# A planned kernel of retention and two mixing layers: waits between GpSimd and VectorE, another load order, another ReLU path, a new plan

## The chip, the cores and the metric

The program runs on one core of one Trainium2 chip. The metric is device time in microseconds of one execution. The profiled execution is one of the same program; its trace gives start and end of every instruction on TensorE (PE, and PEld for its weight loads), VectorE (DVE), ScalarE (ACT), GpSimd (POOL) and the DMA queue that SyncE (SP) issues.

## What is computed

Retention over 768 positions (2 batches, 8 heads of 64), then a layer that mixes positions at low rank and channels with a ReLU between, then a layer with a gate whose other half is normalised and mixed over positions. Shortened:

```python
state = gamma * state + k_t v_t^T            # for t in 768 positions
y_t   = scale * q_t state
x = y as (batch, 768, 512)
u = x + (x^T @ U @ V)^T
x = u + relu(u @ w_ch1) @ w_ch2              # 512 -> 2048 -> 512
h = relu(x @ w_in); a, v = halves of h       # 512 -> 1024
v = (v - mean) / sqrt(var + 1e-6)
out = (a * (w_spatial @ v + b)) @ w_out
```

## The kernel before

The recurrence is done in six chunks of 128 positions. A *pair* is two heads of one batch, eight pairs in all, 0 to 3 of the first batch. For each pair TensorE makes scores (banks `sc`, from keys `k` and queries `q`, both feature-major), which are scaled and masked into `pt`, the chunk sums (`ds`, from token-major keys `kk` and values `v`), and VectorE scans these into states `s`. A masked tile is made in one of two ways: VectorE does it in one operation (line 451), or ScalarE scales (line 448) and GpSimd masks (line 449); the table `VIA` says which of a pair's four tiles (number 2h+e, half h of the positions, head e) go the second way. `x` then adds the products of `pt` and `v`, and of `s` and `q`. The tokens are turned (`t`, copied into `xtok`) for the low-rank product `g`, which is copied to `gt` and multiplied up again (`hu`), and the result is added to `x`.

All the later products are exact to about float32 by splitting: every operand is a high part (rounded by ScalarE) and a low part (a subtraction on VectorE or GpSimd), and each product is three matmuls (`triple`, line 348 for all matmuls). Weights arrive as 64-bit words and are converted in five operations: two on ScalarE (595, 596), two on VectorE (597, 598), one addition on GpSimd (600); then come the high part `hw` (608) and the low part `lw` (609). Activations are `f` (high and low in one tile), `a` in the channel layer. The first products of the channel layer (all but the first of eight blocks of 256 hidden channels), the gate's and the last ones go through a product of 2 by 2 blocks in seven multiplications (`quad`, banks `qa` to `qd`), with sums of weights and of activations; the second products of the channel layer (`acc`) are plain. `pz` are the products over positions, `qv` those of the normalised half, `qo` the last ones.

Nothing is ordered by hand. Every operation is recorded with the engines that may do it, their costs in ns, and a key (its due time in us); `Plan.arrange` goes through time, gives each engine the earliest operation that can start, and chooses between VectorE, GpSimd and ScalarE; `settle` repeats this 14 times with keys moved towards the latest possible times. `give_out` then writes the instructions in the order of planned start. Constants (`AT0`, `LEAD`, `SUM0` and the like) are due times. Each engine runs its list in that order, so an operation that waits holds all behind it on its engine. The planner assumes that VectorE and GpSimd operations marked True, those that read two inputs of SBUF, don't overlap; before, nothing in the program enforced which of the two goes first. Where the plan leaves TensorE idle for over 500 ns, `give_out` writes filler matmuls on a constant; `WARM` fillers start the program. The loads go out on SyncE's queue in the order of `LOADS`: `q`, `h` (the feature-major keys), `k` (the token-major keys), `v`, then `gs`, `U`, `V` and weights; up to eight are in flight. A pair in `TURNED` has no token-major load: TensorE transposes its keys (line 414) and VectorE and ScalarE scale them into `kk` (419).

Of the kernel before, what the change touches and what calls it, by code (L numbers as in the profile page):

```python
# [39 lines left out]
class Op:  # L40
    __slots__ = ("key", "eng", "fn", "bufs", "deps", "outs", "need", "start", "end", "seq", "size", "cost")


class Plan:
# [16 lines left out]
    def op(self, eng, fn, r=(), w=(), key=None, size=0):  # L61

        o = Op()
        o.key, o.eng, o.fn, o.size = (self.key if key is None else key), dict(eng), fn, size
# [28 lines left out]
    def arrange(self, sizes):  # L93
# [15 lines left out]
        dma, sent = 0.0, 0  # L109
        free["D"] = FIRST  # L110
# [17 lines left out]
        def span(o, e, t0):  # L128
# [20 lines left out]
        while given < len(order):  # L149
# [107 lines left out]
    def give_out(self, engines, pools, idle):  # L257

        free = 0.0
        for o in sorted(self.ops, key=lambda o: (o.start, o.seq)):  # L260
# [15 lines left out]
def vss(n):  # L276
    return 152 + 1.03 * n, True
# [22 lines left out]
def pe(n, passes=1):  # L300
    return passes * (10.8 + 0.4219 * n), False
# [3 lines left out]
POOLS = {"a": 36, "w": 24, "raw": 2, "y": 2, "t": 2, "r": 6, "st": 6, "s": 2, "g": 2, "sm": 2, "ps": 8}  # L305
# [5 lines left out]
WARM = 11  # L311
# [3 lines left out]
AT0, AT1, CH0, CH1 = 1.0, 20.7, 43.5, 22.3  # L315
STEP0, STEP1, UV = 4.9, 5.3, 21.6
LOADS = 'q0 h0 v0 k1 gs h1 v1 q1 q2 h2 k2 v2 q3 h3 k3 v3 U V0 V1 w10 w11 q4 h4 k4 v4 w20 w21 q5 h5 v5 k5 q6 k6 v6 q7 h6 v7 h7 k7'.split()
LEAD = 11.1
# [3 lines left out]
SUM0, SUM1 = 80.8, 106.2  # L322
VIA = {0: (2,), 1: (), 2: (), 3: (0, 1, 2, 3), 4: (2, 3), 5: (1, 2, 3), 6: (1, 2), 7: (1, 3)}
# [3 lines left out]
TURNED = (0,)  # L327
# [8 lines left out]
def tile_kernel(ctx: ExitStack, tc: tile.TileContext, a, out: bass.AP):  # L336
    nc = tc.nc
    const = ctx.enter_context(tc.tile_pool(name="const", bufs=1))
    psm = ctx.enter_context(tc.tile_pool(name="psm", bufs=1))
# [16 lines left out]
    sc_t = const.tile([P, 2 * H + NP * (NCH - 1)], F32, name="scales")  # L356
# [71 lines left out]
    def scores(i):  # L428
# [3 lines left out]
        for h in range(2):  # L432
# [8 lines left out]
            op({"P": (690, "keys")}, run, r=[(k_t[i], h), (q_t[i], h)], w=sc)  # L441
# [17 lines left out]
        op({"P": (600, "tokens")}, run, r=[(kk_t[i], 0), (kk_t[i], 1), v_t[i]], w=[ds])  # L459
# [3 lines left out]
    def mix(i):  # L463

        for h in range(2):
# [3 lines left out]
            for z, x in enumerate(xp):  # L469
# [5 lines left out]
                op({"P": (656, "tokens")}, intra, r=[v_t[i + z], (pt_t[i + z, 0], h), (pt_t[i + z, 1], h)], w=[x])  # L475
# [45 lines left out]
    def up(b):  # L521
        for h in range(2):
            for j in range(NP // 2):
# [6 lines left out]
                op({"P": (660, "up")}, run, r=[g_t[b], (vst, h)], w=u)  # L530
# [216 lines left out]
    def ch1(m, b):  # L747
        def store(i, h, src, add=None, y=None):
# [52 lines left out]
    def gate_v(b, c0):  # L801

        sm = Buf("sm", [P, 2, 16], F32, f"sm{b}{c0}")
# [78 lines left out]
    with tc.manual_schedule():  # L882
# [6 lines left out]

        def busy(n):  # L890
# [3 lines left out]
        dma(lambda: sc_t[:], lambda: a["sc"], P * 36 * 4, w=["sc"], eng="E")  # L894
# [7 lines left out]
        op({"A": (1500.0, False)}, lambda e: e.activation(psm.tile([P, 1], F32, name="table"), warm[:, 0:1], AF.Copy))  # L902
# [90 lines left out]
        plan.give_out({"P": None, "V": nc.vector, "A": nc.scalar, "G": nc.gpsimd, "D": nc.sync, "E": nc.scalar}, pools, spend)  # L993
# [70 lines left out]
```

## Time and profile before

| | us |
|---|---|
| three timed runs: lowest, median, highest | 455.47, 455.50, 456.25 |
| the profiled execution | 454.77 |
| its span in the trace | 453.1 |
| TensorE busy (share of the span) | 447.2 (99%) |
| VectorE busy | 396.3 (87%) |
| ScalarE busy | 257.0 (57%) |
| GpSimd busy | 126.7 (28%) |
| data read and written | 39.27 MB, 3.15 MB |

The span is about 1.7 us shorter than the execution it belongs to; the rest lies outside the traced instructions. The ends of matmuls are modelled and each overlaps the next, so a group's duration is a little more than the distance to the next group's start; starts are exact. An engine's idle time counts only where TensorE waits for what the engine makes.

### The profile page before, as it was taken

The numbers are of one execution on the slowest core, as the hardware profiler recorded it, in microseconds if no ns is written. First come the engines' busy times: TensorE is split into PE (matmuls) and PEld (weight loads), VectorE is DVE, ScalarE is ACT, GpSimd is POOL, SyncE is SP. The second block draws the span as 40 slices with busy tenths as digits, with TensorE's granted clock in tenths as the row PEclk, the third lists the DMA queues.
The fourth block names the chain that finished last, engine by engine and source line by source line (L and its number), as shares of the span: only waits on it lengthen the run. The fifth ranks groups of instructions, "written<-read, shape, count | busy, mean of one in ns | idle before, by whom it ended". The sixth has DMA issues, their size and how long they took to land.

```text
span 453.1 us, 8442 instructions
## 1 busy us (share of the span) xinstructions
PE 447.2 (99%) x3235; PEld 434.8 (96%) x3235; DVE 396.3 (87%) x847; ACT 257.0 (57%) x526; POOL 126.7 (28%) x112
## 2 busy tenths in 40 slices
PE   9999999999999999999999999999999999999996
PEld 6888799999999999999999999999999999999996
DVE  2767899999999999989888797899997999999843
ACT  3376775673766675754563554566566778353410
POOL 3076763463834242322131012101410001150000
PEclk9999999999999999999999999999999999999999
DMA  8995412320353341433122012000112022000033
GB/s 299 399 399 192 139 50 93 93 94 10 90 179 95 94 138 50 150 110 107 54 93 81 13 48 87 19 1 1 35 36 72 0 94 93 2 1 1 1 139 139
DMA packets 14151, 42.95 MB, mean 95 GB/s; under 512 B 1696, under 2 KB 2592, under 8 KB 14112
## 3 DMA queue, kind: packets, MB, share of 16 engines
q1 hardware_dynamic: 13968, 42.41, 27.3%
q8 instruction: 25, 0.41, 0.4%
q14 instruction: 14, 0.11, 0.1%
q10 hardware_dynamic: 144, 0.02, 0.0%
HBM read 39.27 MB, written 3.15 MB: 94 GB/s over the span
## 4 chain that ended last, share of the span: by engine, by line
PE 92%; DVE 5%; ACT 1%; POOL 0%; issue 0%; DVEq 0%; ACTq 0%
PE acc L348 29%; PE pz L348 8%; PE x L348 4%; PE c L348 4%; PE sc L348 3%; PE t L502 1%; PE ds L348 1%; DVE s21t L556 1%; DVE f21t L562 1%; PE idle L348 1%; DVE f21b L562 1%; DVE pz L862 1%; DVE x L863 1%; PE q10a L348 1%; PE q50a L348 0%; PE qo11d L348 0%
## 5 line engine op out<-in xcount | busy, mean ns | idle before, releaser
L348 PE MATMUL acc<-a,hw 128*128 128x384 f32 x512 | 130.1, 334 | 0.0
L348 PEld LDWEIGHTS acc<-a,hw 128*128 128x128 f32 x512 | 92.5, 188 | 0.3 <-DVE a L759 0.3
L348 PE MATMUL acc<-a,lw 128*128 128x384 f32 x256 | 85.5, 334 | 0.0
L784 DVE TENSOR_TENSOR x<-acc,x 128x384 f32<-128x384 f32 x128 | 69.3, 550 | 7.5 <-PE acc L348 6.9
L600 POOL TENSOR_TENSOR rw<-rw,tw 128x512 int32<-128x512 int32 x32 | 50.7, 1586 | 82.8 <-DVE rw L598 69.8
L348 PEld LDWEIGHTS acc<-a,lw 128*128 128x128 f32 x256 | 48.1, 188 | 0.0
L757 ACT ACTIVATE y<-y 128x384 f32<-128x384 f32 x42 | 22.0, 523 | 36.9 <-DVE y L756 36.7
L595 ACT ACTIVATE yw<-raww 128x512 f32<-128x512 f32 x32 | 21.6, 676 | 19.7 <-DVE rw L598 15.0
L759 DVE TENSOR_TENSOR a<-y,a 128x384 fp32r<-128x384 f32 x39 | 23.7, 608 | 2.9 <-ACT a L758 2.5
L598 DVE SCALAR_TENSOR_TENSOR rw<-yw,rw 128x512 uint32<-128x512 uint32 x32 | 23.1, 723 | 0.0
L596 ACT ACTIVATE tw<-raww 128x512 int32<-128x512 uint32 x32 | 21.6, 674 | 1.1 <-POOL rw L600 1.0
L600 POOL TENSOR_TENSOR rwo<-rwo,two 128x512 int32<-128x512 int32 x4 | 5.4, 1341 | 60.0 <-DVE rwo L598 60.0
L758 ACT CAST a<-y 128x384 fp32r<-128x384 f32 x42 | 21.5, 513 | 1.0
L449 POOL TENSOR_TENSOR pt<-pt,shared 128x384 f32<-128x384 f32 x14 | 14.2, 1036 | 18.7 <-ACT pt L448 18.6
L348 PE MATMUL pz<-ws,vn 128*128 128x384 f32 x108 | 19.0, 334 | 0.0
L348 PE MATMUL pz<-hws,vn 128*128 128x384 f32 x72 | 18.9, 334 | 0.0
L348 PEld LDWEIGHTS pz<-ws,vn 128*128 128x128 f32 x108 | 18.8, 188 | 0.0
L600 POOL TENSOR_TENSOR rwv<-rwv,twv 128x512 int32<-128x512 int32 x4 | 5.3, 1333 | 30.9 <-DVE rwv L598 12.6
L608 ACT CAST hw<-rw 128x512 fp32r<-128x512 f32 x18 | 11.1, 618 | 4.5 <-POOL rw L600 4.2
L348 PE MATMUL sc<-q,k 64*128 64x128 f32 x192 | 13.4, 281 | 0.0
L597 DVE TENSOR_SCALAR rw<-yw 128x512 uint32<-128x512 uint32 x32 | 13.4, 423 | 0.0
L348 PEld LDWEIGHTS sc<-q,k 64*128 64x128 f32 x192 | 11.7, 187 | 1.6 <-issue 0.7
(1080 smaller groups left out, 1260.6 us busy)
## 6 DMA issues: line engine op xcount, KB each, us to landing
raww<-in_w SPq DMA_DIRECT2D x32, 512.0 KB, 3.6
q<-in_qT SPq DMA_DIRECT2D x8, 384.0 KB, 7.8
k<-in_kT SPq DMA_DIRECT2D x8, 384.0 KB, 7.9
v<-in_v SPq DMA_DIRECT2D x8, 384.0 KB, 7.7
kk<-in_k SPq DMA_DIRECT2D x7, 384.0 KB, 7.8
raws<-in_ws SPq DMA_DIRECT2D x6, 384.0 KB, 3.0
out_y<-out SPq DMA_DIRECT2D x6, 384.0 KB, 2.4
rawwu<-in_wu SPq DMA_DIRECT2D x4, 512.0 KB, 3.5
```

Source lines behind the costliest of these rows:

```text
L348: nc.tensor.matmul(o, l, r, start=start, stop=stop, skip_group_check=True)
L449: op({"G": gss(T)}, lambda E, pt=pt: E.tensor_mul(pt(), pt(), tri()), r=[(pt_t[i, e], h), TRI], w=[(pt_t[i, e], h)])
L595: op({"A": c}, lambda E: E.activation(y.t, words(1).bitcast(F32), AF.Copy, scale=2.0 ** -112), r=whole, w=[y])
L596: op({"A": c}, lambda E: E.activation(t.t, words(0), AF.Copy, scale=2.0 ** -29), r=whole, w=[t])
L597: op({"V": vone(n)}, lambda E: E.tensor_single_scalar(r.t, y.t.bitcast(U32), 3, ALU.logical_shift_left), r=[y], w=[r])
L598: op({"V": vss(n)}, lambda E: E.scalar_tensor_tensor(r.t, y.t.bitcast(U32), 0x80000000, r.t, ALU.bitwise_and, ALU.bitwise_or), r=[y, r], w ...
L600: op({"G": gss(n)}, lambda E: E.tensor_tensor(o().bitcast(I32), r.t.bitcast(I32), t.t, ALU.add), r=[r, t], w=[tok])
L608: op({"A": acp(DM)}, lambda E: E.copy(h.t, f(r.t)), r=[r], w=[h])
L757: op({"A": (525, False)}, lambda E: E.activation(y[0](), y[0](), AF.Relu), r=[y[1]], w=[y[1]])
L758: op({"A": acp(T)}, lambda E: E.copy(t.t[:, 0, :], y[0]()), r=[y[1]], w=[(t, 0)])
L759: op({"V": vss(T), "G": gss(T)}, lambda E: E.tensor_sub(t.t[:, 1, :], y[0](), f(t.t[:, 0, :])), r=[y[1], (t, 0)], w=[(t, 1)])
L784: op({"V": vps(T)}, lambda E, o=o, v=xs(b, d, h): E.tensor_add(v, o.t, v), r=[o, ("X", b, d, h)], w=[("X", b, d, h)])
```

## The change

- A GpSimd operation marked as sharing with VectorE is made to wait for the last such VectorE operation that was planned in front of it, if that one was planned to end less than 3,000 ns ahead (`tie`). The planner also keeps 100 ns (`TIE`) between them, and all costs on VectorE, ScalarE and GpSimd are raised by 1% (`PAD`); some costs on TensorE are set anew.
- Pair 0's keys are the first load, its queries the second; pair 1 joins `TURNED`. The order of the other loads changes. Nine fillers start the program instead of eleven, and the count of later ones is rounded down.
- ReLU in the channel layer: before, ScalarE took the ReLU in place and then rounded the result into the high part, and the low part was a subtraction. Now ScalarE writes the ReLU straight into the high part, and VectorE makes the low part from the unclipped sum, with the ReLU in the same operation.
- The last block is added and stored in two halves, by the queues of ScalarE and SyncE.
- `w` has 23 buffers for 24 and `raw` 3 for 2; due times, `VIA` and so the whole order are new.

```diff
-                st = max(st, port[0])
+                st = max(st, port[0] + (TIE if e == "G" else 0.0))
...
+                    o.tie = sole if e == "G" and sole is not None and sole.end > st - NEARBY else None
+                    sole = o if e == "V" else sole
...
-                    idle(int((o.start - free - 200.0) / 320.0) + 1, target[-1])
+                    idle(int((o.start - free - 100.0) / 320.0), target[-1])
...
-            o.fn(engines[o.eng])
+            o.ins = o.fn(engines[o.eng])
+            if o.eng == "G" and o.cost[1] and o.tie is not None:
+                tie(o.ins, o.tie.ins)
...
-WARM = 11
+WARM = 9
-LOADS = 'q0 h0 v0 k1 gs h1 v1 q1 q2 h2 k2 v2 q3 h3 k3 v3 U V0 V1 w10 w11 ...
+LOADS = "h0 q0 v0 h1 gs q1 v1 q2 h2 v2 k2 h3 k3 q3 v3 U V0 V1 w10 w11 ...
-LEAD = 11.1
+LEAD = 13.9
-VIA = {0: (2,), 1: (), 2: (), ...
+VIA = {0: (2, 3), 1: (1,), 2: (0,), ...
-TURNED = (0,)
+TURNED = (0, 1)
...
-            op({"A": (525, False)}, lambda E: E.activation(y[0](), y[0](), AF.Relu), r=[y[1]], w=[y[1]])
-            op({"A": acp(T)}, lambda E: E.copy(t.t[:, 0, :], y[0]()), r=[y[1]], w=[(t, 0)])
-            op({"V": vss(T), "G": gss(T)}, lambda E: E.tensor_sub(t.t[:, 1, :], y[0](), f(t.t[:, 0, :])), r=[y[1], (t, 0)], w=[(t, 1)])
+            op({"A": (525, False)}, lambda E: E.activation(t.t[:, 0, :], y[0](), AF.Relu), r=[y[1]], w=[(t, 0)])
+            op({"V": vss(T)}, lambda E: E.scalar_tensor_tensor(t.t[:, 1, :], y[0](), 0.0, f(t.t[:, 0, :]), ALU.max, ALU.subtract), r=[y[1], (t, 0)], w=[(t, 1)])
...
+            if (b, m, i, h) == (B - 1, 1, 0, 1):
+                for z, q in enumerate("ED"):
+                    sl, to = slice(z * T // 2, (z + 1) * T // 2), slice(h * T + z * T // 2, h * T + (z + 1) * T // 2)
+                    op({"V": vps(T // 2)}, lambda E, sl=sl, to=to: E.tensor_add(t.t[:, to], src.t[:, sl], add[0]()[:, sl]), r=[src, add[1]], w=[(t, h, z)])
+                    dma(lambda to=to: out[b, d * P:(d + 1) * P, to], lambda to=to: t.t[:, to], P * T * 2, r=[(t, h, z)], eng=q)
...
+        def tie(late, early):
+            tc.add_manual_dep(late.ins, early.ins.name, mybir.DependencyInfo(mybir.DependencyClass.Sync, mybir.DependencyReason.DATA), reason="port")
```

How the order moves is shown at three places. First GpSimd's list at the start, from the copies of the decay factors to pair 3's masks (`pt` with pair and head; before first, then after):

```order
L385 COPY decay1_130<-scales_94 128x320 x2
L449 TENSOR_TENSOR pt00_187<-pt00_187,shared_111 128x384
L449 TENSOR_TENSOR pt30_415<-pt30_415,shared_111 128x384
L449 TENSOR_TENSOR pt31_428<-pt31_428,shared_111 128x384
L449 TENSOR_TENSOR pt30_415<-pt30_415,shared_111 128x384
```

```order
L392 COPY decay1_124<-scales_91 128x320 x2
L456 TENSOR_TENSOR pt00_173<-pt00_173,shared_96 128x384
L456 TENSOR_TENSOR pt01_177<-pt01_177,shared_96 128x384
L456 TENSOR_TENSOR pt11_262<-pt11_262,shared_96 128x384
L456 TENSOR_TENSOR pt20_308<-pt20_308,shared_96 128x384
L456 TENSOR_TENSOR pt30_409<-pt30_409,shared_96 128x384
```

Pair 0 now has two masks on GpSimd, and pairs 1 and 2 one each.

Second, VectorE's list where the second batch's additions of `hu1` meet the first weight tiles of the channel layer (`rw`, `lw10`, `lw11`; `s` and `f` are sums and splits of the first batch's activations):

```order
L533 TENSOR_TENSOR x1_96<-hu112_1008,x1_96 128x384
L533 TENSOR_TENSOR x1_96<-hu113_1009,x1_96 128x384
L609 TENSOR_TENSOR lw10_1059<-rw10_851,hw10_927 128x512
L562 TENSOR_TENSOR f00b121_968<-x0_95,f00b121_968 128x384
L556 TENSOR_TENSOR s00t3_1069<-x0_95 128x384
L562 TENSOR_TENSOR f00b221_974<-x0_95,f00b221_974 128x384
```

```order
L496 COPY xtok30_936<-t70_932 128x3x128
L616 TENSOR_TENSOR lw10_954<-rw10_887,hw10_944 128x512
L604 TENSOR_SCALAR rw20_983<-yw20_908 128x512
L604 TENSOR_SCALAR rw21_987<-yw21_923 128x512
L563 TENSOR_TENSOR s00t1_815<-x0_92 128x384
L605 SCALAR_TENSOR_TENSOR rw20_983<-yw20_908,rw20_983 128x512
L616 TENSOR_TENSOR lw11_1006<-rw11_889,hw11_985 128x512
L540 TENSOR_TENSOR x1_93<-hu100_1001,x1_93 128x384
```

The low part `lw10` stood behind the eight additions and now stands in front of them, as does `lw11`, which was GpSimd's before.

Third, VectorE's list in the last stretch, where the splits of the second batch's sums (`f21t`) end and the first sums of the output blocks (`yo`, from banks `qo`) begin:

```order
L562 TENSOR_TENSOR f21t20_5323<-s21t2_5313,f21t20_5323 128x384
L562 TENSOR_TENSOR f21t21_5362<-s21t2_5313,f21t21_5362 128x384
L562 TENSOR_TENSOR f21t40_5345<-s21t4_5336,f21t40_5345 128x384
L562 TENSOR_TENSOR f21t41_5372<-s21t4_5336,f21t41_5372 128x384
L694 TENSOR_TENSOR yo000_5330<-qo00b_5340,yo000_5330 128x384
L696 TENSOR_TENSOR yo001_5396<-qo00c_5353,yo000_5330 128x384
L873 TENSOR_TENSOR out001_5402<-qo00d_5326,yo001_5396 128x384
```

```order
L569 TENSOR_TENSOR f21t20_5278<-s21t2_5268,f21t20_5278 128x384
L569 TENSOR_TENSOR f21t21_5317<-s21t2_5268,f21t21_5317 128x384
L569 TENSOR_TENSOR f21t41_5327<-s21t4_5291,f21t41_5327 128x384
L701 TENSOR_TENSOR yo000_5285<-qo00b_5295,yo000_5285 128x384
L569 TENSOR_TENSOR f21t40_5300<-s21t4_5291,f21t40_5300 128x384
L703 TENSOR_TENSOR yo001_5351<-qo00c_5308,yo000_5285 128x384
L569 TENSOR_TENSOR f21b210_5170<-x1_93,f21b210_5170 128x384
L890 TENSOR_TENSOR out001_5361<-qo00d_5281,yo001_5351 128x384
```

The sum `yo001` now has one split behind it that stood in front, and one split stands between it and `yo000`.

## Rows read from the trace of the kernel before

**Rows 1.** The page, part 1: busy us (share of the span) xinstructions, by engine
```profile
PE 447.2 (99%) x3235; PEld 434.8 (96%) x3235; DVE 396.3 (87%) x847; ACT 257.0 (57%) x526; POOL 126.7 (28%) x112
```

**Rows 2.** Waits of TensorE's weight loads (PEld): us in total, times, longest
```profile
PEld c L348 <- POOL lw L609: 0.9, 1, 0.9
PEld hu L348 <- DVE gt L489: 0.7, 1, 0.7
...
PEld c L348 <- ACT hw L608: 0.7, 1, 0.7
...
PEld qo00c L348 <- DVE yo L696: 0.5, 1, 0.5
...
PEld qv02c L348 <- DVE yv L696: 0.4, 1, 0.4
...
PEld acc L348 <- DVE a L759: 0.3, 1, 0.3
PEld q10a L348 <- DVE lw11a L609: 0.2, 1, 0.2
```

**Rows 3.** Timeline of TensorE, 0 to 16 us: start, us, engine, line, operation, count
```profile
0.84 3.68 PE L348 MATMUL idle<-const-bfloat16-1.0 128*128 128x384 bf16 x11 [0.84 <-PEq L1053]
...
5.92 1.08 PE L414 MATMUL k<-shared,k 128*128 128x128 f32 x6
6.92 1.61 PE L348 MATMUL sc<-q,k 64*128 64x128 f32 x24
...
10.40 0.88 PE L348 MATMUL x<-pt,v 128*64 128x128 f32 x12
...
13.33 0.50 PE L348 MATMUL sc<-const-bfloat16-1.0 128*128 128x384 bf16 x2
13.77 1.61 PE L348 MATMUL sc<-q,k 64*128 64x128 f32 x24
```

**Rows 4.** DMA issues up to 1.3 us: KB each, median us to landing
```profile
q<-in_qT SPq DMA_DIRECT2D x1, 384.0 KB, 3.1
k<-in_kT SPq DMA_DIRECT2D x1, 384.0 KB, 3.6
```

**Rows 5.** Timeline of ScalarE and GpSimd, 8 to 10.5 us
```profile
8.56 0.58 ACT L448 ACTIVATE pt<-sc,scales 128x384 f32<-128x384 f32 x1 [1.11 <-PE sc L348]
...
9.30 1.00 POOL L449 TENSOR_TENSOR pt<-pt,shared 128x384 f32<-128x384 f32 x1 [3.52 <-ACT pt L448]
```

**Rows 6.** Timeline of TensorE, 56 to 59 us
```profile
56.81 0.59 PE L348 MATMUL c<-f00b,hw 128*128 128x384 f32 x2
57.96 0.44 PE L348 MATMUL c<-f00b,lw 128*128 128x384 f32 x1 [0.56 <-POOL lw L609]
```

**Rows 7.** Chain that ended last, 330 us to the end: start, us, what
```profile
371.04 36.42 PE pz L348 x210
...
407.48 0.57 DVE pz L862
...
424.88 1.88 DVE f21t L562 x4
```

**Rows 8.** Groups by line: names, shapes, count | busy us, mean ns | idle before
```profile
L489 ACT COPY xtok<-t 128x384 f32<-128x384 f32 x11 | 5.0, 481 | 6.6 <-PE t L502 6.5
...
L639 DVE TENSOR_TENSOR lsbw<-sbw,hsbw 128x512 fp32r<-128x512 f32 x7 | 4.8, 681 | 0.0
```

**Rows 9.** Timeline of GpSimd and VectorE, 83.7 to 86 us
```profile
83.73 1.55 POOL L600 TENSOR_TENSOR rw<-rw,tw 128x512 int32<-128x512 int32 x1 [0.63 <-DVE rw L598]
...
84.10 1.74 DVE L609 TENSOR_TENSOR lw11a<-rw,hw11a 128x512 fp32r<-128x512 f32 x1
```

**Rows 10.** The page, part 6: stores, KB each, median us to landing
```profile
out_y<-out SPq DMA_DIRECT2D x6, 384.0 KB, 2.4
out_y<-out SPq DMA_DIRECT2D x4, 192.0 KB, 1.9
```

**Rows 11.** Line 600, GpSimd's addition of 512: count, ns min/median/max
```profile
L600 POOL TENSOR_TENSOR rw<-rw,tw x32: 1284/1348/4427, 49.9 to 228.6; 128x512 int32<-128x512 int32 x32
```

More of the change, by code (lines that the diff above doesn't have):

```diff
@@ L40 @@
 class Op:
-    __slots__ = ("key", "eng", "fn", "bufs", "deps", "outs", "need", "start", "end", "seq", "size", "cost")
+    __slots__ = ("key", "eng", "fn", "bufs", "deps", "outs", "need", "start", "end", "seq", "size", "cost", "tie", "ins")
 class Plan:
@@ L63, in op @@
         o = Op()
-        o.key, o.eng, o.fn, o.size = (self.key if key is None else key), dict(eng), fn, size
+        o.key, o.eng, o.fn, o.size = (self.key if key is None else key), {e: (c * PAD if e in "VAG" else c, x) for e, (c, x) in eng.items()}, fn, size
         deps, bufs = {}, []
@@ L108, in arrange @@
         port, tiles = [0.0, None], False
-        dma, sent = 0.0, 0
-        free["D"] = FIRST
+        dma, sent, sole = 0.0, 0, None
+        free["D"], free["P"] = FIRST, FIRST
         def add(o):
@@ L255, in settle, with give_out @@
             go(best[1])
-    def give_out(self, engines, pools, idle):
+    def give_out(self, engines, pools, idle, tie):
         free = 0.0
@@ L300, in pe @@
 def pe(n, passes=1):
-    return passes * (10.8 + 0.4219 * n), False
+    return passes * (11.3 + 0.4219 * n), False
 NM = NF // 2
-POOLS = {"a": 36, "w": 24, "raw": 2, "y": 2, "t": 2, "r": 6, "st": 6, "s": 2, "g": 2, "sm": 2, "ps": 8}
+POOLS = {"a": 36, "w": 23, "raw": 3, "y": 2, "t": 2, "r": 6, "st": 6, "s": 2, "g": 2, "sm": 2, "ps": 8}
 SLACK = {'P': 0.0, 'V': 100.0, 'A': 150.0, 'G': 300.0, 'D': 30.0}
@@ L314 @@
 DIPS = {3: 450.0, 4: 450.0, 13: 900.0, 22: 300.0, 32: 300.0}
[L315 to L318 removed]
+AT0, AT1, CH0, CH1 = 1.7, 18.3, 49.4, 7.8
+STEP0, STEP1, UV = 3, 4.3, 23.2
+LOADS = "h0 q0 v0 h1 gs q1 v1 q2 h2 v2 k2 h3 k3 q3 v3 U V0 V1 w10 w11 q4 h4 k4 v4 w20 w21 q5 h5 v5 k5 q6 k6 k7 v6 q7 v7 h6 h7".split()
+LEAD = 13.9
 ORDER = '1567243'
@@ L321 @@
 LASTSUMS = "t1=b12-b11 t1 t2=b22-t1 t2 t3=b22-b12 t3 t4=b21-t2 t4"
-SUM0, SUM1 = 80.8, 106.2
-VIA = {0: (2,), 1: (), 2: (), 3: (0, 1, 2, 3), 4: (2, 3), 5: (1, 2, 3), 6: (1, 2), 7: (1, 3)}
+SUM0, SUM1 = 77.5, 95.2
+VIA = {0: (2, 3), 1: (1,), 2: (0,), 3: (0, 1, 3), 4: (0, 1, 2, 3), 5: (0, 3), 6: (1,), 7: (1, 3)}
+HALF = ()
 INPLACE = lambda m, b, i, h: False
 MS = 1
-TURNED = (0,)
+PAD = 1.01
+TIE, NEARBY = 100.0, 3000.0
+TURNED = (0, 1)
 SEQ = [(m, b) for m in range(NM) for b in range(B)]
@@ L354, in dma @@
         op({eng: (55.0, False)}, lambda e: e.dma_start(dst(), src()), r, w, key, size)
-    sc_t = const.tile([P, 2 * H + NP * (NCH - 1)], F32, name="scales")
+    NS = 2 * H + NP * (NCH - 1)
+    sc_t = const.tile([P, NS + 1], F32, name="scales")
     ksc, msc = sc_t[:, 0:H], sc_t[:, H:2 * H]
@@ L440, in run @@
                         mm(sc[e].t[:, c, :], k_t[i].t[r, sl], q_t[i].t[r, sl], True, True)
-            op({"P": (690, "keys")}, run, r=[(k_t[i], h), (q_t[i], h)], w=sc)
+            op({"P": (705, "keys")}, run, r=[(k_t[i], h), (q_t[i], h)], w=sc)
             for e in range(2):
@@ L458, in run @@
                     mm(ds.t[r, :, c], kk_t[i].t[:, c, r], v_t[i].t[:, c, place(i, e)], True, True)
-        op({"P": (600, "tokens")}, run, r=[(kk_t[i], 0), (kk_t[i], 1), v_t[i]], w=[ds])
+        op({"P": (625, "tokens")}, run, r=[(kk_t[i], 0), (kk_t[i], 1), v_t[i]], w=[ds])
         s_t[i] = s = Buf("s", [P, D * (NCH - 1)], F32, f"s{i}")
@@ L529, in run @@
                         mm(u[z].t, g_t[b].t[rows, :], vst.t[rows, h * T:(h + 1) * T], True, True)
-                op({"P": (660, "up")}, run, r=[g_t[b], (vst, h)], w=u)
+                op({"P": (380, "up")}, run, r=[g_t[b], (vst, h)], w=u)
                 for z in range(2):
@@ L901, in tile_kernel @@
         plan.key = -20.0
-        op({"A": (1500.0, False)}, lambda e: e.activation(psm.tile([P, 1], F32, name="table"), warm[:, 0:1], AF.Copy))
+        op({"A": (1500.0, False)}, lambda e: e.activation(sc_t[:, NS:NS + 1], warm[:, 0:1], AF.Copy))
         plan.key = 0.0
```

15 lines of the change are left out of this document (10 added, 5 removed).

## The prediction

> **What bounds the kernel now.** I read the busy shares first: TensorE is busy for 447.2 of 453.1 us, 99% [rows 1]. In this profile a busy TensorE can still be one that is held up, so the second view was what its weight loads waited for; a load that waits holds every matmul behind it. The waits from 50 us on that a new order can reach are few: a weight tile's low part 0.9 us and its high part 0.7, the small product gt 0.7, yo 0.5, yv 0.4, a low part of the activations 0.3 and lw11a 0.2 [rows 2]. The rest is the front, where real work starts 5.92 us into the span behind 16 fillers [rows 3], and the tail behind the last product. What VectorE, ScalarE and GpSimd do elsewhere changes nothing.
>
> The matmul work stays nearly the same. By the order TensorE has the same products in both programs, but for fillers, 21 before and 12 now, and six more transposes of keys (pair 1 joins pair 0 in having its keys turned on the chip).
>
> **The change part by part.**
>
> *Keys of pair 0 first, fewer fillers.* Eleven fillers and, by the order, five more run from 0.84 to 5.92 [rows 3], about 317 ns each for 384 columns; that is 1.2 columns per ns, the lower level of TensorE's clock. The scores from 6.92 take 1.61 us, as do those from 13.77 [rows 3], so by 6.92 the upper level, 2.4 GHz, is there. The queries, issued first, at 0.81, land after 3.1 us, at 3.9; the keys, second, at 1.24, after 3.6, at 4.85 [rows 4]. The transposes need the keys alone, so even before they stood ready a microsecond sooner than the fillers let them in. Now the keys have the first place and land at 3.9, and ten fillers end at 0.84 + 10 x 0.317 = 4.0. Six transposes took 1.00 us across the rise of the clock [rows 3]; wholly at the lower level I estimate 1.3, so to 5.3, when the queries are there too. If the clock rises where it did, near 6.4, the scores do half of 1.1 us' work by then and the other 1.06 us at full speed, and end at 7.5 instead of 8.5: 1.0 us ahead.
>
> It doesn't keep that. In pair 0's second half two products now go over ScalarE and GpSimd, where one did. Before, ScalarE began at 8.56, GpSimd's product took 1.00 us from 9.30 [rows 5], and TensorE went on at 10.40 [rows 3]: 1.84 us after ScalarE's start. With another 1.00 us behind it that is 2.84, so 7.5 + 2.84 = 10.3. The six new transposes (at most 1.00) and the one filler lie in this wait and cost nothing while it lasts; without it they would cost up to 1.0. From there the same three groups follow as before, which ended at 13.33 and now end at 13.25. Before, two fillers follow to 13.77 [rows 3], a wait for pair 2's keys; one load fewer stands ahead of these now (pair 1's token-major keys), so that wait goes. **Term: -0.45 us.** Bounds: -1.1 if GpSimd's second product doesn't hold TensorE, +0.5 if the clock rises only after the scores.
>
> *The passage to the channel layers.* Before, the first channel product began at 56.81, did two matmuls and stood until 57.96 for the second weight tile's low part, which GpSimd had [rows 6]; a matmul of 384 columns takes 36.42 / 210 = 0.173 [rows 7], so it stood 0.8 us. Now both low parts are on VectorE in front of the second batch's eight additions, and their weights are loaded earlier (a third raw buffer, a place ahead of the last pair's keys). The 0.8 us should go. The wait for the high part overlaps with that for a bank, which stays, so I count nothing for it. Against this, the products hu010 to hu013, which stood between the last transposes and g1, have moved ahead of the second batch's mixing, and nothing covers the copy of the last transpose any more: 0.48 [rows 8] and about 0.1 of hand-over, so +0.6. The wait for gt stays; its copy moves to ScalarE, behind three weight operations. **Term: -0.2**, between -0.9 and +0.9.
>
> *The order in the normalised half.* TensorE waited 0.4 us for yv [rows 2], with three independent matmuls between the two uses of the bank qv02c. Now fifteen stand there, of some 0.12 us each (0.173 for 384 columns [rows 7], here 256). 1.4 us more cover hides 0.4. **Term: -0.4**, at worst 0.
>
> *The last stretch.* From the addition at 407.48, whose product TensorE had just ended, VectorE runs without a break until yo is done at 427.9: 42 operations, of which four take 1.88 us, 0.47 each [rows 7]; TensorE waits 0.5 for it [rows 2]. In the new order 37 operations stand between the same two, 17.4 us. More work stands in front, and VectorE may come to the place 1.2 us late (20 operations, 10.6 us by such paces, against three groups of 18 matmuls, 9.4). 1.2 + 17.4 is still 1.8 us under 20.4, so VectorE has idle time and nothing new is late. **Term: -0.5**, at worst 0.
>
> *GpSimd waits for VectorE.* While GpSimd ran an addition from 83.73 to 85.28, VectorE's operation lw11a started at 84.10 and took 1.74 us [rows 9], against 0.68 for this shape undisturbed [rows 8]; the load behind it waited 0.2. The activations' 0.3 goes back to a like case. So such blocks do reach TensorE, but for 0.5 us in all [rows 2]; the others are covered. **Term: -0.45.** The wait is GpSimd's; behind it only GpSimd's own operations are queued, mostly weights, whose conversion is now planned 2.8 us earlier (the lead in the diff), and that covers it.
> A rule bears on this: the Trainium skill ("SBUF — State Buffer", section "Who interferes with whom") says that a VectorE instruction with two SBUF inputs and a GpSimd instruction that reads SBUF exclude each other for the whole instruction, and that the order of issue decides who blocks. Rows 9 agree: VectorE's operation ended 0.56 after GpSimd's. By that rule the wait guards the one operation that it names and not the next, and the term could be 0.
>
> *ReLU straight to the high part.* 42 casts on ScalarE go, and three low parts move from GpSimd to VectorE. No load of TensorE in rows 2 waits for such a cast alone; it is worth slack and no time.
>
> *The tail.* The last store, 192 KB, lands 1.9 us after its issue, and one of 384 KB took 2.4 [rows 10], so most of it doesn't go with the bytes. Halved over two queues, the second half's addition ends when the whole one did. **Term: 0**, -0.2 to +0.2.
>
> **Sum.** -0.45 - 0.2 - 0.4 - 0.5 - 0.45 = -2.0. A fresh order has waits of its own; the old one has 1.4 us of them behind 60 us (0.5 + 0.4 + 0.3 + 0.2 [rows 2]), and I put a fifth of that back, 0.3. So -1.7. The profiled execution took 454.8 us with a span of 453.1, the three timed runs 455.5 in the median; taken off the median: **453.8 us**.
>
> **The rivals.**
> *More is won.* GpSimd's second product lies beside other work (-0.65 more), g1 finds its data in time (-0.6), no new wait comes (-0.3): 452.2. For it: each needs only that one engine runs a little earlier than I placed it; against: in the new order nothing independent stands in those two gaps.
> *The same, with new holes.* The front's lead is eaten by the transposes (+0.45), the wait doesn't keep VectorE free (+0.45), and the new order's waits are as large as the old one's, not a fifth (+0.5 of the 1.1 left): 455.2, no change that can be told.
> *Slower: a late GpSimd product in the attention.* Six splits of the first batch and one sum now stand on GpSimd ahead of the last pair's masks; before there were four splits. An addition on GpSimd takes 1,284 ns at best, 1,348 in the median and 4,427 at worst [rows 11]. One such case there is 3.1 us; the masks feed the last mixing product, and state, transposes, g1 and all of the second batch follow. It decides from the point where the last mask comes after TensorE has done the products in front of it. 453.8 + 3.1 = 456.9. For it: these operations now wait for VectorE too; against: no mask stands among the waits from 50 us on.
>
> **How the numbers follow.** My forecast (452.8 to 454.8) has 0.46, more won 0.16, the same with new holes 0.24, slower 0.14. Runs of this kernel can tell 0.2%, 0.9 us, from no change: faster is below 454.6, slower above 456.4. A little of the forecast's own share ends above 454.6: faster 0.61, same 0.25, slower 0.14. The range leaves out the end of the slow rival and of the best: 451.7 to 456.2.
>
> **What would show it.** Front: transposes from about 4.0, the first scores ended near 7.5, pair 2's scores from 13.3. Passage: no wait for lw, but one of about 0.6 for xtok in front of g1. Normalised half and last stretch: no wait for yv or yo. Blocks: VectorE's longest low part well under 1.7 us. I am wrong if a mask (pt) holds TensorE for a microsecond or more, or if the first scores start later than 5.5.

## The result and the profile after

| | before | after |
|---|---|---|
| timed runs: lowest, median, highest (us) | 455.47, 455.88, 456.80 | 451.00, 451.36, 451.83 |
| profiled execution, its span | 454.77, 453.1 | 451.47, 449.7 |
| ratio after/before, 95% interval | | 0.9899 [0.9879, 0.9918] |

The changed kernel is 4.5 us faster by the medians and 3.3 us by the two profiled executions. The forecast of 453.8 had the sign, but too little of the size: 451.36 lies 0.3 us below its range. Line numbers of the changed kernel are 6 to 17 higher than those of before (matmuls are L354, GpSimd's addition of 512 is L607, VectorE's low part of a weight L616).

The page of the changed kernel: busy us (share of the span) and instructions by engine; the shares of the chain that ended last; GpSimd's largest group (busy, mean ns | idle before).

```profile
PE 444.0 (99%) x3232; PEld 434.4 (97%) x3232; DVE 395.7 (88%) x843; ACT 241.6 (54%) x488; POOL 114.5 (25%) x117
...
PE 97%; DVE 1%; ACT 1%; issue 0%; DVEq 0%; ACTq 0%
...
L607 POOL TENSOR_TENSOR rw<-rw,tw 128x512 int32<-128x512 int32 x32 | 41.0, 1292 | 111.4 <-DVE rw L605 72.2
```

Against [rows 1], GpSimd has 12 us less of busy time with as many operations of its main kind (the 32 additions take 1,292 ns in the mean, and the slowest 1,302, where [rows 11] had 4,427), and ScalarE 15 us less. The chain that ended last is now TensorE nearly throughout.

What TensorE's weight loads wait for, after (us in total, times, longest):

```profile
PEld hu L354 <- ACT gt L496: 0.9, 1, 0.9
...
PEld c L354 <- DVE x L540: 0.6, 1, 0.6
```

Of [rows 2], the waits for lw, hw, yo, yv, a and lw11a have all gone, and the waits that are left lie in front of 56 us; that for gt, now ScalarE's copy, is 0.2 us longer. Timeline of TensorE, after, at the front and at the passage to the channel layer (start, us, engine, line, what, count [idle before]):

```profile
4.00 1.49 PE L421 MATMUL k<-shared,k 128*128 128x128 f32 x6
5.41 1.70 PE L354 MATMUL sc<-q,k 64*128 64x128 f32 x24
7.71 0.80 PE L354 MATMUL ds<-v,kk 128*64 128x64 f32 x20 [0.60 <-DVE pt L458]
...
9.11 0.87 PE L421 MATMUL k<-shared,k 128*128 128x128 f32 x6
...
10.07 0.88 PE L354 MATMUL x<-pt,v 128*64 128x128 f32 x12
...
13.26 1.61 PE L354 MATMUL sc<-q,k 64*128 64x128 f32 x24
```

```profile
51.73 1.52 PE L354 MATMUL g<-xtok,ust 128*32 128x128 f32 x48
53.18 0.34 PE L354 MATMUL hu<-const-bfloat16-1.0 128*128 128x384 bf16 x1
54.21 1.57 PE L354 MATMUL hu<-vst,gt 32*128 32x384 f32 x16 [0.70 <-ACT gt L496]
55.77 0.62 PE L354 MATMUL c<-f00b,hw 128*128 128x384 f32 x2
56.23 0.34 PE L354 MATMUL c<-f00b,lw 128*128 128x384 f32 x1
56.40 0.51 PE L354 MATMUL c<-f00b,hw 128*128 128x384 f32 x2
```

**Where the 3.39 us between the two spans lie** (453.06 and 449.67, unrounded). Pair 2's scores begin at 13.26, where they began at 13.77 [rows 3]: 0.51. The fourth channel matmul begins at 56.40; before, the third began at 57.96 [rows 6] and the fourth at 58.24, so 1.84 in all, of which 1.33 lie between 13.3 and the channel layer. Behind 60 us I took the distance of each matmul to the next, less 0.173 (0.12 where it has 256 columns): before, five places had 0.10, 0.18, 0.25, 0.43 and 0.50 too much (at 70.4, 85.6, 208, 353 and 427), after, none has more than 0.07. That is 1.46. From the last matmul's end to the span's end it is 3.49 and 3.45. 1.84 + 1.46 + 0.04 = 3.34 of 3.39.

Of the 1.33 us, 0.8 is the wait for lw. Most of the rest lies in the last pair's scores, before (start, us):

```profile
43.39 0.29 PEld L348 LDWEIGHTS sc<-q,k 64*128 64x128 f32 x2 [0.20 <-ACT pt L448]
43.39 2.07 PE L348 MATMUL sc<-q,k 64*128 64x128 f32 x24
...
43.86 1.41 PEld L348 LDWEIGHTS sc<-q,k 64*128 64x128 f32 x22 [0.17 <-ACT pt L448]
```

and after:

```profile
43.58 1.61 PE L354 MATMUL sc<-q,k 64*128 64x128 f32 x24
```

Before, the scores were held twice by ScalarE's scaling of masked tiles, and took 0.46 us longer. The 1.33 repeats: from pair 2's first score to the fourth channel matmul it is 44.46 to 44.48 us in the three profiles of the kernel before, of which two follow below, and 43.15 to 43.18 in three of the changed kernel. Where pair 2's scores begin differs more from one execution to the next: 13.52 to 14.21 before, 13.26 to 13.65 after.

The other 1.1 us between the medians is in none of these places; the runs under "Two more profiles" find it.

### The profile page after: what moved, and what is told of

The parts are those of the page before. It is cut to its first block, busy times and chain, and to the rows that moved or that the text cites. A ratio compares the mean times of both kernels' runs of the same rounds, so it can differ in the third digit from the quotient of the medians.

```text
span 449.7 us, 8409 instructions
## 1 busy us (share of the span) xinstructions
PE 444.0 (99%) x3232; PEld 434.4 (97%) x3232; DVE 395.7 (88%) x843; ACT 241.6 (54%) x488; POOL 114.5 (25%) x117
## 4 chain that ended last, share of the span: by engine, by line
PE 97%; DVE 1%; ACT 1%; issue 0%; DVEq 0%; ACTq 0%
PE acc L354 30%; PE pz L354 11%; PE c L354 4%; PE x L354 3%; PE sc L354 3%; PE ds L354 1%; PE t L509 1%; PE hu L354 1%; PE idle L354 1%; PE qu00c L354 0%; PE qu11d L354 0%; PE qo11d L354 0%; PE qu11c L354 0%; PE qu01a L354 0%; PE k L421 0%; PE qo11c L354 0%
## 5 line engine op out<-in xcount | busy, mean ns | idle before, releaser
L354 PE MATMUL acc<-a,hw 128*128 128x384 f32 x512 | 129.8, 334 | 0.0
L354 PEld LDWEIGHTS acc<-a,hw 128*128 128x128 f32 x512 | 92.5, 188 | 0.0
L354 PE MATMUL acc<-a,lw 128*128 128x384 f32 x256 | 85.5, 334 | 0.0
L607 POOL TENSOR_TENSOR rw<-rw,tw 128x512 int32<-128x512 int32 x32 | 41.0, 1292 | 111.4 <-DVE rw L605 72.2
L354 PEld LDWEIGHTS acc<-a,lw 128*128 128x128 f32 x256 | 48.0, 188 | 0.0
L769 ACT ACTIVATE a<-y 128x384 fp32r<-128x384 f32 x42 | 22.0, 525 | 36.0 <-DVE y L763 34.3
L770 DVE SCALAR_TENSOR_TENSOR a<-y,a 128x384 fp32r<-128x384 f32 x42 | 23.5, 559 | 0.9 <-ACT a L769 0.6
L456 POOL TENSOR_TENSOR pt<-pt,shared 128x384 f32<-128x384 f32 x16 | 15.7, 1005 | 14.9 <-ACT pt L455 12.9
L354 PE MATMUL pz<-ws,vn 128*128 128x384 f32 x108 | 19.0, 334 | 0.0
L354 PE MATMUL pz<-hws,vn 128*128 128x384 f32 x72 | 18.9, 334 | 0.0
L354 PEld LDWEIGHTS pz<-ws,vn 128*128 128x128 f32 x108 | 18.7, 188 | 0.0
L616 DVE TENSOR_TENSOR lw<-rw,hw 128x512 fp32r<-128x512 f32 x18 | 12.7, 706 | 0.6 <-ACT hw L615 0.6
L855 POOL TENSOR_TENSOR ve<-r,ve 128x128 fp32r<-128x128 f32 x7 | 3.1, 461 | 39.0 <-DVE vn L855 20.1
L354 PEld LDWEIGHTS pz<-hws,vn 128*128 128x128 f32 x72 | 13.1, 188 | 0.0
L354 PE MATMUL sc<-q,k 64*128 64x128 f32 x192 | 12.7, 280 | 0.0
L354 PEld LDWEIGHTS sc<-q,k 64*128 64x128 f32 x192 | 11.4, 189 | 1.3 <-issue 0.5
```

The source lines that it names most:

```text
L354: nc.tensor.matmul(o, l, r, start=start, stop=stop, skip_group_check=True)
L456: op({"G": gss(T)}, lambda E, pt=pt: E.tensor_mul(pt(), pt(), tri()), r=[(pt_t[i, e], h), TRI], w=[(pt_t[i, e], h)])
L607: op({"G": gss(n)}, lambda E: E.tensor_tensor(o().bitcast(I32), r.t.bitcast(I32), t.t, ALU.add), r=[r, t], w=[tok])
L616: op({"V": vss(DM), "G": gss(DM)}, lambda E: E.tensor_sub(l.t, f(r.t), f(h.t)), r=[r, h], w=[l])
L769: op({"A": (525, False)}, lambda E: E.activation(t.t[:, 0, :], y[0](), AF.Relu), r=[y[1]], w=[(t, 0)])
L770: op({"V": vss(T)}, lambda E: E.scalar_tensor_tensor(t.t[:, 1, :], y[0](), 0.0, f(t.t[:, 0, :]), ALU.max, ALU.subtract), r=[y[1], (t, 0)], ...
```

## The experiments

My first theory, from the two traces, was that the new order carries the gain (1.84 us ahead of the channel layer, four waits gone) and that GpSimd's waits guard GpSimd. The rival was that these waits carry it. Kernels that were timed together ran on one chip and share the runs of the kernel before, which had a median of 455.5 to 455.7 us on three chips and of 454.56 on one; so I compare within a chip, and where that can't be done the text says so.

### The waits taken out, and the waits alone

```diff
             o.ins = o.fn(engines[o.eng])
-            if o.eng == "G" and o.cost[1] and o.tie is not None:
-                tie(o.ins, o.tie.ins)
```

> The changed kernel with the waits of GpSimd for VectorE taken out; every instruction stands where it stood on its engine. First theory (the new order on TensorE carries the gain, the waits guard GpSimd alone): 451.4 to 452.0 us against 451.4 of the changed kernel, that is at most the 0.45 us of the prediction's term; GpSimd's 128x512 weight conversions become uneven again (single ones of 3 us and more), no wait of TensorE over 0.3 us comes back after 60 us, and the channel layer still begins at 55.8. Rival (the waits carry it: GpSimd shut out or shutting out VectorE held TensorE in places that move from run to run): 453 to 455 us, with waits of TensorE for the split halves or for the sums again.

The reverse, the kernel before with these lines and the record of the VectorE operation that they need, and nothing else:

> The kernel before with the waits of GpSimd for VectorE put in, in its own order of instructions, and nothing else of the change. First theory: 455.0 to 456 us against 455.5 to 455.9, since the two waits of TensorE between 52.9 and 58.0 (xtok, lw) and the four after 60 us have other causes; of these at most the 0.18 us for lw11a goes. Rival: 452 to 453.5 us.

Measured, beside 455.54 of the kernel before: without the waits 453.52 us (453.30 to 454.02; ratio 0.9950 [0.9936, 0.9963]), the waits alone 454.80 (454.35 to 455.39; 0.9975 [0.9958, 0.9991]). The first theory misses both. On the new order the waits are worth some 2.1 us, nearly half of the whole gain (the changed kernel had 451.36 elsewhere, and on this chip 451.29 with its last store in one piece), and on the old one 0.7. The rival's 453 to 455 holds for the first, but for the second it gave 452 to 453.5: the waits need the new order to be worth that much.

What the weight loads wait for without the waits:

```profile
PEld qo00c L352 <- DVE yo L701: 1.2, 1, 1.2
...
PEld qu10a L352 <- ACT yu L494: 0.5, 1, 0.5
```

These two make 1.15 and 0.47 of matmul distance, 1.6 of the 2.13 us between the two spans. The rest isn't traced to the waits. The channel layer begins 0.17 later, all of it in front of pair 2's scores (13.42), within what differs there from one execution to the next. And the end takes 0.30 longer, behind the last store, between GpSimd's closing semaphore instructions; three runs below have the same 0.3 to 0.4, and its cause is open. From pair 2's first score to the fourth channel matmul it is 43.14 without the waits: that part of the gain is the order's alone.

The wait for yo, which the new order was to end, is back and larger than in [rows 2]. Its cause stands 20 us ahead of it, as the run with the last waits alone confirms. VectorE and GpSimd without the waits, 402 to 409 us:

```profile
403.39 1.51 DVE L644 TENSOR_TENSOR lsbwo<-sbwo,hsbwo 128x512 fp32r<-128x512 f32 x1
404.82 1.37 DVE L567 TENSOR_TENSOR f20t<-s20t,f20t 128x384 fp32r<-128x384 f32 x1
406.11 1.37 DVE L567 TENSOR_TENSOR f21b<-x,f21b 128x384 fp32r<-128x384 f32 x1
407.40 1.02 DVE L871 TENSOR_TENSOR pz<-pz,bb 128x384 f32<-128x384 f32 x2
...
402.82 2.95 POOL L561 TENSOR_TENSOR s20t<-x,s20t 128x384 f32<-128x384 f32 x2 [5.66 <-DVE s20t L561]
405.73 2.61 POOL L567 TENSOR_TENSOR f20t<-s20t,f20t 128x384 fp32r<-128x384 f32 x2
```

The same operations in the changed kernel:

```profile
402.91 0.68 DVE L646 TENSOR_TENSOR lsbwo<-sbwo,hsbwo 128x512 fp32r<-128x512 f32 x1
403.51 0.55 DVE L569 TENSOR_TENSOR f20t<-s20t,f20t 128x384 fp32r<-128x384 f32 x1
403.98 0.55 DVE L569 TENSOR_TENSOR f21b<-x,f21b 128x384 fp32r<-128x384 f32 x1
404.45 1.02 DVE L873 TENSOR_TENSOR pz<-pz,bb 128x384 f32<-128x384 f32 x2
405.38 1.01 DVE L874 TENSOR_TENSOR x<-pz,x 128x384 f32<-128x384 f32 x2
...
404.67 1.99 POOL L563 TENSOR_TENSOR s20t<-x,s20t 128x384 f32<-128x384 f32 x2 [7.80 <-PE pz L354]
406.63 1.99 POOL L569 TENSOR_TENSOR f20t<-s20t,f20t 128x384 fp32r<-128x384 f32 x2
```

Without the waits GpSimd's four operations start at 402.82, as soon as their data are there. They run beside three VectorE operations that take both inputs from SBUF, and each of those takes 0.82 us longer (1.51 against 0.68, 1.37 against 0.55 twice): 2.5 us in all. With the wait they start behind f21b at 404.67 (the row names `pz` as what ended the idle time, but the wait is all that differs between the two runs) and run beside additions and products of which one input is the PSUM bank `pz`. There VectorE keeps 0.47 us from one to the next, and each of GpSimd's four takes 1.0 us instead of 1.3 to 1.5. So the wait doesn't remove the meeting of the two engines. It moves it to VectorE operations that don't mind. The Trainium skill ("SBUF — State Buffer", section "Who interferes with whom") says that a VectorE instruction with at most one input in SBUF, outside its two-port modes, uses ports of its own, and that with two inputs in SBUF it excludes a reading GpSimd instruction; both halves of that stand in these rows.

### Only the waits of the last stretch

```diff
-            if o.eng == "G" and o.cost[1] and o.tie is not None:
+            if o.eng == "G" and o.cost[1] and o.tie is not None and o.start > 400000.0:
```

> The changed kernel with only the waits of GpSimd for VectorE behind 400 us left in, in front of all the four sums and splits of f20t and s20t; all other waits are out, every instruction stands where it stood. Theory (of the 2.1 us that the waits were worth, about 1.4 lie at this one place: without them these four run beside three VectorE operations in SBUF and lengthen each by 0.83 us, and the wait for yo at 426 costs 1.15 us and the end 0.3): 452.0 to 452.4 us, no wait for yo, the wait of 0.5 us for yu at 309 stays. Rival (VectorE is late at 402 already, from blocks before it): 453.2 to 453.6 us with the wait for yo.

Measured: 452.21 us (451.81 to 452.85), on the chip where the kernel before has 454.56. What TensorE waits for behind 60 us:

```profile
PE qu10a L354 <- ACT yu L496: 0.2, 1, 0.2
```

The wait for yo is gone and that for yu stays, as the theory says; so the waits at this one place give the 1.15 us back. The medians differ by 1.3 from the run without waits, but that one was on another chip. The end keeps its 0.3, so this isn't from the blocks at 402 us. In this profile 0.47 us is lost in the attention instead, which the run without waits didn't lose, though neither has waits there. The changed kernel itself was not timed on this chip, from which the runs with the old due times and the old ReLU path are too; on others it had 451.4 to 451.5.

### Two more profiles: what the first one didn't have

Before the next two runs I had the 3.3 against 4.5 us open. The first is the kernel before, unchanged:

> The kernel before, once more under the profiler, since its profiled execution (454.77 us) lies 0.5 to 2 us below all its timed runs. First theory (GpSimd and VectorE meet at other places in each execution): 455.3 to 456.2 us, and the 0.5 to 1.4 us more lie in waits of TensorE for split halves, low parts or sums behind VectorE operations that were held up. Rival: they lie in the loads of the first 20 us, and everything behind 60 us stands as in the first profile.

454.31 us, a miss: as short as the first profile, and its four longest waits behind 60 us have 0.19, 0.25, 0.43 and 0.46, the same as there. So the meetings seemed fixed. But this chip is the one on which the median of the kernel before is a microsecond lower (454.56, from 454.30 to 455.45), so I took it once more on another chip, beside the changed kernel:

> The changed kernel once more, beside the kernel before on the same chip, since the distance of the two medians (4.5 us) is larger than that of their two profiled executions (3.3 us). First theory (the distance of the traces is the true one, the rest is the chip on which each was timed): about 3.3 us below the kernel before, ratio 0.992 to 0.994. Rival (the kernel before loses 1 us more in its usual execution than in the profiled one): ratio 0.989 to 0.991.

> The kernel before under the profiler, on the same chip as the changed kernel above. First theory: its waits behind 60 us stand where they stood in the first two profiles (85, 208, 353, 427 us; 1.3 to 1.4 us together), and what differs between executions lies in front of 20 us, behind the values and masks of the first pairs. Rival: the four waits differ by 0.3 us or more in sum.

The changed kernel had 451.48 us (451.24 to 452.02), the kernel before 455.66 (455.13 to 455.95), ratio 0.9908 [0.9891, 0.9925], which reaches into both theories' ranges and decides nothing; the profile of before does. It took 455.98 us; the four waits stand where they stood (0.17, 0.25, 0.42 and 0.47), as the first theory says, but there is another long one, which neither theory named. Its rows around 118 us, VectorE, GpSimd and TensorE:

```profile
118.14 1.52 DVE L634 TENSOR_TENSOR qw<-rw,qw 128x256 fp32r<-128x256 f32 x1
119.58 0.68 DVE L639 TENSOR_TENSOR lsbw<-sbw,hsbw 128x512 fp32r<-128x512 f32 x1
...
117.77 1.61 POOL L600 TENSOR_TENSOR rw<-rw,tw 128x512 int32<-128x512 int32 x1 [1.55 <-DVE rw L598]
...
119.91 0.34 PE L348 MATMUL acc<-a,hw 128*128 128x384 f32 x1
120.78 0.44 PE L348 MATMUL acc<-a,hw 128*128 128x384 f32 x1 [0.53 <-DVE a L759]
121.06 0.33 PE L348 MATMUL acc<-a,lw 128*128 128x384 f32 x1
```

And the same place in the first profile of before:

```profile
117.70 0.42 DVE L634 TENSOR_TENSOR qw<-rw,qw 128x256 fp32r<-128x256 f32 x1
118.03 0.69 DVE L639 TENSOR_TENSOR lsbw<-sbw,hsbw 128x512 fp32r<-128x512 f32 x1
...
117.32 4.43 POOL L600 TENSOR_TENSOR rw<-rw,tw 128x512 int32<-128x512 int32 x1 [1.55 <-DVE rw L598]
```

In the first profile VectorE's operations went ahead, one behind the other, and GpSimd's addition lasted 4.43 us: it is the 4,427 of [rows 11]. The second profile has the same (4,423 ns). In this one GpSimd got in ahead of qw, which took 1.52 us instead of 0.42, and the low part behind it held TensorE for 0.70 + 0.10 us (0.87 and 0.28 from start to start, less 0.173 each). The two executions differ by 1.18 us of span: 0.80 here, and 0.44 by which the channel layer starts later. The same program thus has two outcomes at 118 us, and the profile on which the prediction rests showed the one that is free for TensorE. The same section of the Trainium skill says that the order of issue, not the shape of an operation, decides who is held. These rows don't show it decided by the order of the starts: GpSimd's addition starts 0.37 to 0.38 us ahead of qw in both executions, while the VectorE operation in front of qw still runs. What makes GpSimd win in one and lose in the other stays open. The kernel before with the waits alone has no such wait, and its 0.74 us is about the size of this one. The second profile is from the chip with the low median and the third from one with a high median; that this outcome is what separates them would fit, but it was not traced run by run.

On this chip the spans are 454.24 and 449.99. The fourth channel matmul begins 1.97 earlier (56.71 against 58.68), and behind 60 us 2.1 us of waits are gone; with 0.04 of the end that is 4.15 of 4.25.

### The parts of the order: first loads, due times, ReLU, last store

```diff
-LOADS = "h0 q0 v0 h1 gs q1 ...
+LOADS = "q0 h0 v0 h1 gs q1 ...
```

> The changed kernel with the queries of pair 0 loaded ahead of its keys again, the plan made anew around that. First theory (term of the front -0.45 us): the six transposes of pair 0 stand in front of the first scores again with nothing to hide in, pair 2's scores begin at 13.7 instead of 13.3, and the time is 451.7 to 452.3 us. Rival (the loads of pair 0 are hidden, since the masks and the values land later than both): 451.2 to 451.6 us. A new hole of the fresh order elsewhere could add to either; it would show as a wait behind 20 us.

Measured: 451.75 us (450.50 to 451.97) beside 455.54. That is within the first theory's range. But it is only 0.3 to 0.4 us above the changed kernel's medians, less than the spread of its own runs, so a cost of the old load order isn't shown. The channel layer begins at 56.03; in three profiles of the changed kernel it begins at 55.77, 56.06 and 56.19. Timeline of TensorE:

```profile
5.63 0.85 PE L421 MATMUL k<-shared,k 128*128 128x128 f32 x6 [0.77 <-DMA k<-in_kT]
6.41 1.61 PE L354 MATMUL sc<-q,k 64*128 64x128 f32 x24
...
10.26 1.61 PE L354 MATMUL sc<-q,k 64*128 64x128 f32 x24
```

The first scores come a microsecond later, as expected, and yet pair 1's scores come earlier (10.26 against 10.88). Pair 2's come at 14.50, later than the 13.7 expected, and pair 3's at 19.50, where the changed kernel has 19.48. So the microsecond by which the first scores differ is gone by pair 3.

The plan's due times as before the change:

```diff
-AT0, AT1, CH0, CH1 = 1.7, 18.3, 49.4, 7.8
-STEP0, STEP1, UV = 3, 4.3, 23.2
+AT0, AT1, CH0, CH1 = 1.0, 20.7, 43.5, 22.3
+STEP0, STEP1, UV = 4.9, 5.3, 21.6
...
-LEAD = 13.9
+LEAD = 11.1
...
-SUM0, SUM1 = 77.5, 95.2
+SUM0, SUM1 = 80.8, 106.2
```

> The changed kernel with the eleven numbers of the plan's due times (attention, channel layer, steps, sums, UV and LEAD) as they were before the change, all else as changed. First theory (the order itself carries about half of the gain, and these numbers set it): 452.5 to 454.5 us, with waits of TensorE in attention or in the last stretch. Rival (the waits make any fresh order even): 451.2 to 451.8 us.

Measured: 454.27 us (453.57 to 454.70) beside 454.56, ratio 0.9988 [0.9979, 0.9997]: nearly the whole gain gone, with all else of the change in place. TensorE at the passage:

```profile
56.23 1.57 PE L354 MATMUL hu<-vst,gt 32*128 32x384 f32 x16 [0.16 <-ACT gt L496]
58.71 0.62 PE L354 MATMUL c<-f00b,hw 128*128 128x384 f32 x2 [0.91 <-DVE x L540]
```

The channel layer begins 2.9 us later than in the changed kernel (58.71 against 55.77), 2.5 of it behind pair 2's first score (45.66 us to the fourth channel matmul against 43.15), and behind 60 us there is no wait over 0.1 us; the end takes 0.3 longer. The loss is in the attention and its passage.

The old ReLU path, for all 42 parts:

```diff
-HALF = ()
+HALF = tuple((i, h) for i in range(2) for h in range(2))
```

> The changed kernel with the old ReLU path in all 42 low parts of the first product: ReLU to y, a copy of its own to the high part, a subtraction that GpSimd may take; the plan made anew around that. First theory (the prediction's 0 for this term, ScalarE has room): 451.2 to 451.8 us with ScalarE's busy time up by about 42 x 0.51 = 21 us from 241.6. Rival (the shorter way to the low part is what took the short waits out of the row): 452.2 to 453.5 us, with waits of TensorE for a between 100 and 260 us.

Measured: 452.52 us (452.09 to 452.96) beside 454.56, in the rival's range, but its waits aren't where the rival put them. ScalarE has its 42 casts back (21.6 us); TensorE's longest waits behind 60 us are new ones, 0.4 us for a split half at 308 and this one at 346:

```profile
PE qv01c L354 <- DVE yv L703: 0.2, 1, 0.2
```

Between 100 and 260 us one place has 0.08. So the shorter path wins nothing at the place where it stands; without it the plan comes out with other holes, 0.8 us of them. That is a property of this plan, and another set of due times might have none. The end takes 0.4 longer, again behind the last store.

```diff
-            if (b, m, i, h) == (B - 1, 1, 0, 1):   # two halves, two queues
+            if False:
```

> The changed kernel with its last output block summed in one operation and stored in one transfer, as before the change; the instructions of TensorE and GpSimd stand where they stood. First theory (the tail is worth nothing: 3.49 us from the last matmul to the end before, 3.45 after): 451.3 to 451.5 us. Rival (the split shortens the store, and other parts of the tail got longer): 451.6 to 451.9 us.

Measured: 451.29 us (450.93 to 451.83), and 3.43 us from the last matmul to the end. The split store is worth nothing.

### A copy moved: what is left

```diff
...
+        for o in self.ops:
+            if o.eng == "A" and any(d.name == "g1" for d in o.bufs):
+                o.start = min(o.start, max(x.end for x in o.deps) - 600.0)
...
```

Two other numbers of the plan were altered with it (a load's lead, a due time's offset); the instructions stand in the same order on every engine but for the copy and the undivided store.

> The changed kernel with one copy moved: on ScalarE the copy of g1 to gt1 stands in front of the second conversion tw (0.67 us) instead of behind it; the last output block is summed and stored in one piece. Theory (what is left of waiting in the changed kernel lies in front of 56 us, and the 0.7 us that TensorE stands before hu of batch 1 is ScalarE's conversion): the wait before hu falls to 0.2 us, the channel layer begins 0.5 us earlier, and the time is 0.4 to 0.6 us below the changed kernel's on the same chip. Rival (the conversion, now later, makes lw late, and TensorE stands in the channel layer instead): the same time within 0.2 us, with a wait for lw or hw between 56 and 62 us.

> The changed kernel, on the same chip as the run above and as the kernel before. Theory: 4.2 us below the kernel before where that one stands 0.8 us for a low part at 120 us in its usual execution, some 3.2 us below it on a chip on which it does not; its own time between 451.2 and 451.9 us on any chip, and no wait of TensorE over 0.1 us behind 60 us.

Measured on one chip: 451.00 us (450.21 to 451.22) with the copy moved, 451.37 (451.20 to 452.03) for the changed kernel, 455.65 for the one before (ratios 0.9893 [0.9877, 0.9910] and 0.9903 [0.9886, 0.9920]). ScalarE and TensorE with the copy moved:

```profile
53.30 0.29 ACT L499 COPY gt<-g 128x128 f32<-128x128 f32 x1
53.46 0.71 ACT L606 ACTIVATE tw<-raww 128x512 int32<-128x512 uint32 x1
...
53.14 0.34 PE L357 MATMUL hu<-const-bfloat16-1.0 128*128 128x384 bf16 x1
53.64 1.57 PE L357 MATMUL hu<-vst,gt 32*128 32x384 f32 x16 [0.16 <-ACT gt L499]
55.20 0.62 PE L357 MATMUL c<-f00b,hw 128*128 128x384 f32 x2
```

From the filler behind g1 to the channel layer it is 2.06 us where the changed kernel takes 2.59, and no wait comes in its place. The theory holds in the trace, by 0.53 us. The medians differ by 0.37, just under its 0.4 and less than one kernel's own spread, so the times alone don't show it. The changed kernel is 4.28 below the kernel before, with no wait over 0.07 us behind 60 us, as its theory says for a chip of the high median.

What was not timed by itself: the ways of the masks (`VIA`), pair 1's turned keys, the third `raw` buffer, and the 1% and 100 ns of the planner.

## Why the prediction was too small

The forecast of 453.8 was 2.4 us above the 451.36. By the traces 1.1 of this is the passage term and 0.2 the new order's own waits, which didn't come; 0.7 is what the profile of before lay under its median, which the wait of 0.8 at 118 us fits. The other terms came within 0.1 of their sizes. So two steps failed: the passage's sum of a gain and a new wait, and the price of the blocks between GpSimd and VectorE, read from one profile.

- **Keys first, -0.45.** It measured -0.51 in the first two profiles, with transposes from 4.00 and the masked half at 10.07, near the 10.3 worked out. In part that is luck. The scores ended at 7.1, not 7.5. TensorE's upper level (2.4 GHz) was there during them, earlier than the 6.4 I had taken over from before: the 24 scores took 1.70 us, against 1.61 at full speed. That won nothing, since the chunk sums stood until 7.71, here for VectorE (0.60). In the two later profiles of the changed kernel they stood until 8.01 and 8.10 for the load of the values (1.42 and 0.93), which the term doesn't have, and pair 2's scores begin at 13.54 and 13.65.
- **Passage, -0.2.** The term that was mis-sized most: it measured -1.33. The wait for lw went, 0.8, as I said. The 0.6 for xtok in front of g1 never came: g1 starts at 51.73 with the first halves of the transposes, while the copies of the others run beside it. Of the remaining 0.5, 0.46 is the last pair's scores, for which I had no term. The run with the old due times shows that this stretch is where the order has its value, 2.5 us.
- **Normalised half and last stretch, -0.4 and -0.5.** Both waits went, 0.43 and 0.50. The reason was half right. I counted VectorE's operations at their undisturbed pace; without GpSimd's waits the same 37 operations come too late, since 2.5 us of blocks lie in front of them, and TensorE waits 1.15 for yo.
- **GpSimd's waits, -0.45.** This step failed. I priced them by the waits of before that a block had caused, 0.5 us in the rows. Those went, 0.43 us. But what the waits are worth is what the new order would lose without them: 2.1 us by the times, 1.6 by the trace. The reading of the rule that gave 0 failed too: it is true that VectorE is still held by GpSimd here and there in the changed kernel (single weight operations of 1.6 us at 225, 256 and 272), but at places with cover.
- **Off which time.** I took a difference of two profiles off the median of the timed runs. The profile of before lay 0.7 under that median, and I noted it and went on. It lacked the 0.8 us at 118, which the third profile of before has and none of the three of the changed kernel.
- **ReLU 0, tail 0, own waits of the new order +0.3.** The tail is 0. The ReLU path is 0 where it stands, and some 0.8 us by the plan that it allows. New waits behind 60 us there were none.

Of the rivals, "more is won" at 452.2 came nearest, and it had two of the three reasons: g1 finds its data in time, and no new wait comes. No mask held TensorE for a microsecond, and no late GpSimd product showed.

## What to carry to other kernels

Where two engines share something, a single operation of 4.43 us among others of 1.29 can be the harmless half of a race: ask what the program loses when the other side wins, and take more profiles, on another chip too, before a difference is taken off a median. A wait that costs nothing on an idle engine can choose what its operation runs beside; put GpSimd's work beside VectorE operations that read PSUM. Price such a wait by what the new order would lose without it, not by what the old one lost. And compare distances inside one execution rather than starts: from pair 2 to the channel layer three executions of one kernel agreed to 0.03 us, while pair 2's own start differed by up to 0.7.

## What the runs showed of the hardware that I had not expected

- Beside VectorE operations with one input in PSUM four GpSimd operations took 1.0 us each and VectorE kept 0.47 us between starts; beside operations with both inputs in SBUF the same four took 1.3 to 1.5 us and VectorE lost 0.82 us on each of three.
- The same instructions at the same place gave 4.43 us on GpSimd and no delay on VectorE in one execution, and 1.61 us on GpSimd and 1.1 us of delay on VectorE in another, with GpSimd starting 0.37 to 0.38 us ahead in both.
- The kernel before had a median of 454.56 us on one chip and of 455.54 to 455.66 on three others; the changed kernel had 451.36 to 451.48 in three sets of runs.
- With the same instructions in the same order, TensorE's chunk sums at the start of the changed kernel waited 0.93 and 1.42 us for the load of the values in two executions, and for VectorE (0.60) in another.
